# Splitting the AV product of two head pairs around the scores, and one burst's delay for batch 0's stores

## The chip, the cores and the metric

The kernel runs on one core of one Trainium2 chip. The metric is the device time of one execution in microseconds (us), and the figure quoted for a kernel is the median of its runs.

## The reference

For 8 batches, 12 heads, 448 positions and a head size of 64, attention without softmax is followed by a layer norm without bias, a feed-forward block and a residual. Cut to what matters:

```
scores = q @ k.T / sqrt(64)
attn   = maximum(scores, 0)**2 / 448
x      = attn @ v                      # heads side by side: [8, 448, 768]
xn     = (x - mean) / sqrt(var + 1e-6) * g_ln
out    = x + maximum(xn @ w_ch1, 0) @ w_ch2      # 768 -> 3072 -> 768
```

## The kernel before, in words

Heads are worked on in pairs, six pairs to a batch. The 48 pairs are numbered through, so that batch 2 holds pairs 12 to 17. The scores of one pair are made transposed, with keys on the partitions: three full tiles of 128 keys (t = 0, 1, 2) and a rest of 64 keys, the quarter (t = NF = 3). The quarters of two neighbouring pairs share one tile. `att_QK` makes one tile of scores on TensorE and takes it through the relu into SBUF; `att_square` squares it on VectorE; AV then multiplies the squares by v.

The attention of batch b+1 is computed while the feed-forward of batch b runs. `ffn_1_all(b)` makes the 24 hidden tiles (index `ni`) of the first layer, each 12 matmuls into one PSUM bank, taken out by a relu on ScalarE (L424). After chosen tiles, named in `bursts` (for b of 2 and more at ni = 1, 4, 7, 10, 13, 16, 19; for b = 1 two tiles later; for b = 0 `IN_FIRST`), an `excursion(3)` is put in: it makes the scores of the next three tiles of the list `slots`. When both pairs of a neighbouring couple are complete, that excursion begins with their AV: `att_AV2`. This happens twice for each of the seven batches whose attention lies in a feed-forward, so 14 times in a run. The third couple of a batch is finished by single `att_AV` calls.

The order on every engine is the order in which the Python code emits instructions (`tc.manual_schedule`); nothing reorders them. So what is emitted earlier stands earlier in the queue of its engine, and in SyncE's queue of DMA issues too.

[...] Two score tiles `sc0`, `sc1` of two banks each take turns; `f0` and `f1` (`next_f`) take turns for the feed-forward's tiles and for the AV; `f2` and `f3` are `spare`. The profile writes `f` for all four of f0 to f3. The feed-forward tile just ahead of an `att_AV2` goes to `spare[1]` (f3), so that f0 and f1 are both free for the AV sums of the two pairs. The feed-forward tile after the burst goes to the bank of the first pair, the one after that to the bank of the second. The third tile of scores of a burst (m = 2) is put into f2 and f3, half by half, and its relu is done in two instructions (L295): both on VectorE, or for b = 1 the first on ScalarE (L293) and the second on VectorE.

TensorE is used in tiled shapes, which the profile gives behind the operation: 128\*64 for AV full tiles (L317), the feed-forward (L422) and the Strassen-like second layer (L490); 64\*64 for AV quarters (L341) and score quarters (L284); 64\*128 for full score tiles (L289).

Before the change `att_AV2` does the 6 full-tile matmuls of the first pair, the 6 of the second, then 2 quarter matmuls for each; then `av_out` takes the first pair's sum out on VectorE (L351) and the second's on ScalarE (L349). `av_out` also emits an addition into `xs` on VectorE (L358, L360), and for odd pairs the load of v for the next batch.

q and k of batches 2 and up are loaded by GpSimd DMAs into a ring of three (`load_qk`) and turned by a DMA transpose that SyncE issues (`att_T`, L256) into one of three `qkT` buffers. When the last score tile of pair i has been made, `queued(i)` issues the transpose for pair i + 3 and notes the load for pair i + 6; the loads are issued at the start of the next excursion (`flush_loads`). SyncE also issues all the stores of the output (L450). The output of batch 0 is made by plain products, `plain_part`, whose stores are kept in `held_stores`: 4 tiles, each two DMAs, are let out in `ffn_1_all(1)` behind an excursion.

Of the kernel before, what the change touches and what calls it, by code (L numbers as in the profile page):

```python
# [11 lines left out]
def kernel(  # L12
# [10 lines left out]
    nc = tc.nc  # L23
# [14 lines left out]
    NF = S // P  # L38
    SF = NF * P
    SS = S - SF  # L40
# [93 lines left out]
    def v_parts(b):  # L134
        v_sb = v1_sb if b == 1 else v_ring
        return (v_sb[:, :H * NF * D].rearrange("p (h e) -> p h e", h=H),
                v_sb[:, H * NF * D:].rearrange("p (a e) -> p a e", a=NPAIR))
# [21 lines left out]
    def row0(i, hh):  # L159

        return D * ((i + hh) % 2)
# [11 lines left out]
    def load_v(i):  # L173

        b, a = divmod(i, NPAIR)
        v_heads, v_rest = v_parts(b)
        nc.gpsimd.dma_start(v_heads[:, 2 * a:2 * a + 4],
                            v[b, 2 * a:2 * a + 4, :SF].rearrange("h (p t) d -> p h (t d)", t=NF))
        for r0, h0, step in ((0, 0, 3), (D, 1, 1)):
            heads = slice(h0, h0 + step + 1, step)  # L180
            nc.gpsimd.dma_start(v_rest[r0:r0 + SS, a:a + 2, r0:r0 + D],  # L181
                                v[b, 2 * a:2 * a + 4][heads, SF:].rearrange("h s d -> s h d"))
# [33 lines left out]
    attn = {}  # L216
# [4 lines left out]
    def by_j(x):  # L221
        return x.rearrange("p (j s) -> p j s", j=NJ)
# [21 lines left out]
    def q_of(i, r):  # L244
        if i < PE_T * NPAIR:
            return by_j(flat(i)[r, :S])
        return qkT[i][r, :NJ, :SP]

    def k_of(i, r, t, keys):
        c0 = (S if i < PE_T * NPAIR else NJ * P) + t * P  # L250
        return flat(i)[r, c0:c0 + keys]
# [18 lines left out]
            pe_T(i, t, ps)  # L270
        (copy or nc.vector.tensor_copy)(flat(i)[:, :2 * S], ps)

    def att_QK(i, t, relu_by=nc.scalar):

        at = attn_pool.tile([P, 2, S], bf16, tag="attn")
        attn[i, t] = at
        ps = next_sc() if relu_by is nc.scalar else None
        half = [bank[:, :S] for bank in (spare if ps is None else (ps[:, 0], ps[:, 1]))]
        if t == NF:
            for x in range(2):  # L280
                for hh in range(2):
                    r = slice(hh * D, (hh + 1) * D)
                    r0 = row0(i + x, hh)
                    nc.tensor.matmul(by_j(half[x][r0:r0 + SS]), k_of(i + x, r, t, SS), q_of(i + x, r),  # L284
                                     start=True, stop=True)
        else:
            for hh in range(2):
                r = slice(hh * D, (hh + 1) * D)
                nc.tensor.matmul(by_j(half[hh]), k_of(i, r, t, P), q_of(i, r), start=True, stop=True)  # L289
        if ps is None:  # L290
            for x in range(2):
                if relu_by[x] is nc.scalar:
                    nc.scalar.activation(at[:, x], half[x], Act.Relu)  # L293
                else:
                    nc.vector.tensor_scalar(at[:, x], half[x], 0.0, None, op0=Alu.max)  # L295
        else:
            nc.scalar.activation(at, ps[:, :, :S], Act.Relu)  # L297

    def att_square(i, t):
        nc.vector.tensor_mul(attn[i, t], attn[i, t], attn[i, t])  # L300
# [5 lines left out]
    def xT_of(b, ki):  # L306
        return xT[:, ki, (b % 2) * S:(b % 2 + 1) * S]

    def av_part(ps, i, t, start, stop):
        b, pr = divmod(i, NPAIR)  # L310
        v_heads, v_rest = v_parts(b)
        for hh in range(2):
            if t < NF:
                weights, values = v_heads[:, 2 * pr + hh, t * D:(t + 1) * D], attn[i, t][:, hh, :]
            else:
                weights, values = v_rest[:, pr, row0(i, hh):row0(i, hh) + D], attn[i - i % 2, NF][:, i % 2, :]
            nc.tensor.matmul(ps[hh * D:(hh + 1) * D, :], weights, values, start=start, stop=stop)  # L317
# [12 lines left out]
    def att_AV2(i):  # L330

        ps = [next_f()[:, :S] for _ in range(2)]
        for x in range(2):
            for t in range(NF):
                av_part(ps[x], i + x, t, t == 0, False)
        b, pr = divmod(i, NPAIR)
        v_rest = v_parts(b)[1]
        for x in range(2):
            for hh in range(2):
                r0 = row0(i + x, hh)  # L340
                nc.tensor.matmul(ps[x][hh * D:(hh + 1) * D, :], v_rest[r0:r0 + SS, pr + x, r0:r0 + D],  # L341
                                 attn[i, NF][r0:r0 + SS, x, :], start=False, stop=True)
        for x in range(2):
            av_out(i + x, ps[x], (nc.vector, nc.scalar)[x])

    def av_out(i, ps, evac_by):
        b, pr = divmod(i, NPAIR)
        if evac_by is nc.scalar:
            nc.scalar.mul(xT_of(b, pr), ps, c2)  # L349
        else:  # L350
            nc.vector.tensor_scalar(xT_of(b, pr), ps, c2, None, op0=Alu.mult)  # L351
        if i >= PE_T * NPAIR and i % 2 and i + NPAIR < NP_ALL:
            load_v(i - 1 + NPAIR)
        if b == 0:
            if pr < GAIN_FIRST:
                nc.vector.tensor_scalar(xc[:, pr, :], xT_of(b, pr), g_sb[:, pr:pr + 1], None, op0=Alu.mult)
        elif pr == 1:
            nc.vector.tensor_add(xs, xT_of(b, 0), xT_of(b, 1))  # L358
        elif 1 < pr < NPAIR - 1:
            nc.vector.tensor_add(xs, xs, xT_of(b, pr))  # L360
# [101 lines left out]
    held_stores = []  # L462
# [134 lines left out]
    def flush_loads():  # L597
        while loads:
            load_qk(loads.pop(0))

    def queued(i):
        if PE_T * NPAIR <= i + 3 < NP_ALL:
            att_T(i + 3)
            if i + 6 < NP_ALL:
                loads.append(i + 6)
# [12 lines left out]
    ready = []  # L618

    def ends(i, t):  # L620

        if i % 2 == 0:
            return [i] if t == (NF - 1 if i % NPAIR else NF) else []
        return [i] if t == NF - 1 else []

    def next_AV(**how):
        if ready:
            att_AV(ready.pop(0), **how)

    def excursion(n, third=(nc.vector, nc.vector), **how):  # L630
        flush_loads()
        if len(ready) > 1:
            assert ready[0] % 2 == 0 and ready[1] == ready[0] + 1
            att_AV2(ready.pop(0))
            ready.pop(0)
        elif ready and ready[0] % NPAIR == NPAIR - 2:
            next_AV(**how)
        took = [slots.pop(0) for _ in range(n)]
        for m, (i, t) in enumerate(took):
            att_QK(i, t, relu_by=third if m == 2 else nc.scalar)  # L640
        for i, t in took:
            att_square(i, t)
        for i, t in took:
            for e in ends(i, t):
                ready.append(e)
                queued(e)
# [78 lines left out]
    def ffn_1_all(b):  # L725
        ms = tiles_of(b)
        for ni in range(NI0 if b == 0 else 0, K2):
            if b == 0 and ni == NI0:
                ffn_1_first()
            if b == 0 and ni == X_AT[0]:  # L730

                nc.sync.dma_start(held, h[:1, ni - 1, CARRY:CARRY + 16])
            if b == 0 and ni in X_AT:
                ffn_x(b, X_AT.index(ni))
            if b == 0 and ni in V_AT:
                load_v(V_AT[ni])
            bursts = IN_FIRST if b == 0 else [n + (2 if b == 1 else 0) for n in IN_REST]
            ffn_1(ni, spare[1] if b < B - 1 and ni in bursts and len(ready) > 1 else None)
            flush()
            at = STATS_AT[min(b, 2)][:len(ms)]  # L740
            if ni in at:
                ffn_stats(ms[at.index(ni)])
            if b == 1 and ni in SUMS_AT:
                w2_sums(*LATE_SUMS[SUMS_AT.index(ni)])
            if b == 0:
                if ni in IN_FIRST:
                    excursion(3)
                if ni == IN_FIRST[-1] + 3:
                    next_AV(bank=spare[1])
                if ni in T_IN_FIRST:  # L750
                    att_T(NPAIR + T_IN_FIRST[ni])
            elif b < B - 1:
                if ni in bursts:
                    excursion(3, **(dict(third=(nc.scalar, nc.vector), evac_by=nc.scalar) if b == 1 else {}))
                    while ni > bursts[0] and held_stores:
                        held_stores.pop(0)()
                if ni == min(bursts[-1] + 3, K2 - 1):
                    flush_loads()
                    next_AV(bank=spare[1])
# [69 lines left out]
    with tc.manual_schedule(engines=set(ENGINES)):  # L829
# [22 lines left out]
        i = PE_T * NPAIR  # L852
# [41 lines left out]
```

## Time and profile before

| what | value |
|---|---|
| median of 12 runs | 524.38 us (lowest 523.77) |
| profiled execution, its own time | 525.16 us |
| its span in the profile | 523.4 us |
| TensorE matmul busy | 514.5 us (98%) |
| VectorE, ScalarE, GpSimd busy | 368.2, 276.1, 222.6 us |
| granted TensorE clock | 1.0 throughout |

The span runs from the first to the last instruction that the profile shows; 1.8 us of the profiled execution lie outside it. A matmul's end in the profile is modelled, so that "busy" hides small stalls of TensorE: the starts of successive matmuls are the sharper reading. A pair of matmuls in the two halves of a 128\*64 array starts every 0.19 us, although each is shown to take about 0.35 us.

### The profile page before, as it was taken

How to read it: one execution, taken by the hardware profiler on the slowest of the kernel's cores; microseconds unless marked ns; L12 is line 12 of the kernel's file. 1: busy time of each engine (PE TensorE's matmuls, PEld its weight loads, DVE VectorE, ACT ScalarE, POOL GpSimd, SP SyncE). 2: the span in 40 equal slices, each digit the busy share in tenths (PEclk: the TensorE clock that was granted, in tenths of full speed). 3: DMA queues.
4: the chain of work that ended last, by engine and by line, in shares of the span. 5: the costliest groups of instructions: out<-in, count | busy, mean ns of one | idle time of the engine just before them, and what ended most of it. 6: DMA issues, size and time to landing. Idle time of an engine off the chain costs nothing.

```text
span 523.4 us, 13642 instructions
## 1 busy us (share of the span) xinstructions
PE 514.5 (98%) x5705; PEld 318.8 (61%) x5705; DVE 368.2 (70%) x650; ACT 276.1 (53%) x456; POOL 222.6 (43%) x255
## 2 busy tenths in 40 slices
PE   8999999999999999999999999999999999999996
PEld 4445566556765566655787556655666556665665
DVE  5966779778958669587685867787695866951255
ACT  6985643776247652476624766476524765234320
POOL 8727116667523853238532386237532000320031
PEclk9999999999999999999999999999999999999999
DMA  9999999999645992659924599369924300250022
GB/s 141 189 196 203 184 202 164 179 135 107 88 103 73 130 91 63 121 63 130 92 62 105 64 126 137 77 73 119 93 68 100 59 4 3 62 116 7 1 54 69
DMA packets 175261, 53.03 MB, mean 101 GB/s; under 512 B 154208, under 2 KB 175200, under 8 KB 175200
## 3 DMA queue, kind: packets, MB, share of 16 engines
q0 software_dynamic: 103552, 25.74, 53.0%
q1 hardware_dynamic: 71120, 26.06, 27.2%
q8 instruction: 44, 0.72, 0.6%
q10 hardware_dynamic: 528, 0.37, 0.2%
q14 instruction: 17, 0.14, 0.1%
HBM read 51.91 MB, written 11.01 MB: 120 GB/s over the span
## 4 chain that ended last, share of the span: by engine, by line
PE 90%; DVE 5%; DMA 2%; ACT 1%; POOL 1%; issue 0%; POOLq 0%; DVEq 0%
PE f L422 41%; PE f L490 34%; PE f L317 5%; PE f L473 3%; PE sc L289 3%; DVE xT L351 2%; DVE at L300 2%; PE f L289 1%; DMA qkT_t<-qk_ring 1%; DMA w<-in_k_dram 1%; PE f L341 1%; PE f L708 1%; PE f L232 1%; PE f L381 1%; ACT at L297 0%; PE sc L284 0%
## 5 line engine op out<-in xcount | busy, mean ns | idle before, releaser
L422 PE MATMUL f<-xc,w 128*64 128x448 bf16 x2256 | 225.9, 353 | 1.6
L422 PEld LDWEIGHTS <-w 128*64 128x64 bf16 x2256 | 131.5, 110 | 90.3 <-issue 18.7
L424 ACT ACTIVATE h<-f 128x448 bf16<-128x448 f32 x188 | 102.8, 547 | 98.3 <-PE f L422 97.4
L490 PE MATMUL f<-w,s_sb 128*64 128x384 bf16 (+2 forms) x1584 | 130.0, 324 | 0.0
L490 PEld LDWEIGHTS <-s_sb 128*64 128x64 bf16 x1584 | 92.9, 110 | 34.4
L297 ACT ACTIVATE at<-sc 128x896 bf16<-128x896 f32 x120 | 103.3, 918 | 5.0 <-PE sc L289 4.8
L300 DVE TENSOR_TENSOR at<-at 128x896 bf16<-128x896 bf16 x168 | 95.5, 618 | 4.3 <-ACT at L297 4.1
L523 POOL TENSOR_TENSOR o_t<-o_t,x_tok 128x384 f32<-128x384 f32 x26 | 24.4, 938 | 151.6 <-ACT o_t L522 151.6
L169 POOL DMA_DIRECT2D qk_ring<-in_q_dram x36 | 44.5, 1236 | 89.2 <-DMA qkT_t<-qk_ring 63.5
L295 DVE TENSOR_SCALAR at<-f 128x448 bf16<-128x448 f32 x89 | 51.6, 618 | 26.9 <-PE f L289 26.9
L522 ACT ACTIVATE o_t<-f,rstd 128x384 f32<-128x384 f32 x26 | 15.1, 582 | 94.6 <-DVE acc_t L527 35.8
L484 DVE TENSOR_TENSOR s_sb<-h 128x1536 bf16<-128x1536 bf16 x65 | 64.1, 1002 | 0.0
L170 POOL DMA_DIRECT2D qk_ring<-in_k_dram x36 | 53.5, 1487 | 11.0 <-DMA w<-in_moe_w_ch_dram 11.0
L490 PE MATMUL f<-w,h 128*64 128x384 bf16 x624 | 52.9, 326 | 0.0
L171 POOL DMA_DIRECT2D qk_ring<-in_k_dram x36 | 43.9, 1220 | 5.7 <-DMA w<-in_moe_w_ch_dram 4.7
L490 PEld LDWEIGHTS <-h 128*64 128x64 bf16 x624 | 36.9, 110 | 14.1
L351 DVE TENSOR_SCALAR xT<-f 128x448 bf16<-128x448 f32 x33 | 20.4, 619 | 32.3 <-PE f L341 21.8
L523 POOL TENSOR_TENSOR acc_t<-acc_t,x_tok 128x384 f32<-128x384 f32 x24 | 28.9, 1211 | 22.3 <-ACT acc_t L522 21.2
L181 POOL DMA_DIRECT2D v_ring<-in_v_dram x36 | 34.7, 1331 | 0.0
L317 PE MATMUL f<-at,v_ring 128*64 128x448 bf16 x288 | 33.8, 354 | 0.5 <-DVE xT L351 0.3
L388 DVE SCALAR_TENSOR_TENSOR xc<-f,g_sb,xc 128x448 bf16<-128x448 f32 x45 | 28.5, 678 | 6.7 <-PE f L381 6.0
L289 PE MATMUL sc<-qkT_t 64*128 64x448 bf16 x192 | 30.0, 356 | 0.0
(87 smaller groups left out, 394.9 us busy)
## 6 DMA issues: line engine op xcount, KB each, us to landing
w<-in_moe_w_ch_dram POOLq DMA_DIRECT2D x6, 768.0 KB, 12.8
w<-in_moe_w_ch_dram POOLq DMA_DIRECT2D x4, 1152.0 KB, 29.3
v_ring<-in_v_dram POOLq DMA_DIRECT2D x21, 192.0 KB, 5.3
qk_ring<-in_q_dram POOLq DMA_DIRECT2D x36, 112.0 KB, 4.9
qk_ring<-in_k_dram POOLq DMA_DIRECT2D x36, 96.0 KB, 5.0
out_dram<-o_t SPq DMA_DIRECT2D x8, 168.0 KB, 2.2
out_dram<-acc_t SPq DMA_DIRECT2D x7, 168.0 KB, 2.2
out_dram<-o_t SPq DMA_DIRECT2D x8, 144.0 KB, 2.1
```

Of the source, the lines that this page charges most:

```text
L169: nc.gpsimd.dma_start(q_to, q[b, heads].rearrange("x (p j) d -> p j x d", j=NJ))
L170: nc.gpsimd.dma_start(k_to[:, :NF], k[b, heads, :SF].rearrange("x (p t) d -> p t x d", t=NF))
L289: nc.tensor.matmul(by_j(half[hh]), k_of(i, r, t, P), q_of(i, r), start=True, stop=True)
L295: nc.vector.tensor_scalar(at[:, x], half[x], 0.0, None, op0=Alu.max)
L297: nc.scalar.activation(at, ps[:, :, :S], Act.Relu)
L300: nc.vector.tensor_mul(attn[i, t], attn[i, t], attn[i, t])
L317: nc.tensor.matmul(ps[hh * D:(hh + 1) * D, :], weights, values, start=start, stop=stop)
L422: nc.tensor.matmul(ps[c * D:(c + 1) * D, :], w1[:, ki, n0:n0 + D], xc[:, ki, :], start=(ki == 0), stop=(ki == K1 - 1))
L424: nc.scalar.activation(h[:, ni, CARRY:], ps, Act.Relu)
L484: nc.vector.tensor_tensor(s_sb[:, n], x, y, op=op)
L490: nc.tensor.matmul(ps[c * D:(c + 1) * D, :d1 - d0], stat[:, ki, c * D:(c + 1) * D], w2[:, slot, ki, d0:d1], start=(start and ki == 0), sto ...
L523: nc.gpsimd.tensor_tensor(o_t, o_t, x_half(m, dh), op=Alu.add)
```

## The change

Of the two pairs in `att_AV2`, only the first gets its full tiles ahead of the quarters. The quarters of both pairs follow; for the second pair they now begin the sum (`start` is set for x = 1) where they ended it. The first pair's sum is taken out by ScalarE. The rest, the second pair's 6 full-tile matmuls and its `av_out` on VectorE, is returned as a function. The excursion hands it to the `att_QK` of its third tile, which calls it between the two relu instructions. So TensorE does the second pair's full tiles behind all three score tiles, and VectorE takes the sum out between the two halves of the relu.

Apart from that, in `ffn_1_all(1)` the held stores of batch 0 come behind the third burst (ni = 9), where they came behind the second (ni = 6).

```diff
-    def att_QK(i, t, relu_by=nc.scalar):
+    def att_QK(i, t, relu_by=nc.scalar, between=None):
...
                     nc.vector.tensor_scalar(at[:, x], half[x], 0.0, None, op0=Alu.max)
+                if x == 0 and between:
+                    between()
...
     def att_AV2(i):

         ps = [next_f()[:, :S] for _ in range(2)]
-        for x in range(2):
-            for t in range(NF):
-                av_part(ps[x], i + x, t, t == 0, False)
+        for t in range(NF):
+            av_part(ps[0], i, t, t == 0, False)
...
                 nc.tensor.matmul(ps[x][hh * D:(hh + 1) * D, :], v_rest[r0:r0 + SS, pr + x, r0:r0 + D],
-                                 attn[i, NF][r0:r0 + SS, x, :], start=False, stop=True)
-        for x in range(2):
-            av_out(i + x, ps[x], (nc.vector, nc.scalar)[x])
+                                 attn[i, NF][r0:r0 + SS, x, :], start=x == 1, stop=x == 0)
+        av_out(i, ps[0], nc.scalar)
+
+        def rest():
+            for t in range(NF):
+                av_part(ps[1], i + 1, t, False, t == NF - 1)
+            av_out(i + 1, ps[1], nc.vector)
+
+        return rest
...
     def excursion(n, third=(nc.vector, nc.vector), **how):
         flush_loads()
+        rest = None
         if len(ready) > 1:
             assert ready[0] % 2 == 0 and ready[1] == ready[0] + 1
-            att_AV2(ready.pop(0))
+            rest = att_AV2(ready.pop(0))
...
         for m, (i, t) in enumerate(took):
-            att_QK(i, t, relu_by=third if m == 2 else nc.scalar)
+            att_QK(i, t, relu_by=third if m == 2 else nc.scalar, between=rest if m == 2 else None)
...
-                    while ni > bursts[0] and held_stores:
+                    while ni > bursts[1] and held_stores:
                         held_stores.pop(0)()
```

## The prediction

> **What bounds the kernel now.** I read the page first (who is busy, what the chain that ended last consists of), then the chain in order of time, then the timeline of single bursts, and last SyncE's timeline, because the change also moves stores.
>
> ```profile
> span 523.4 us, 13642 instructions
> ...
> PE 514.5 (98%) x5705; PEld 318.8 (61%) x5705; DVE 368.2 (70%) x650; ACT 276.1 (53%) x456; POOL 222.6 (43%) x255
> ...
> PEclk9999999999999999999999999999999999999999
> ...
> PE 90%; DVE 5%; DMA 2%; ACT 1%; POOL 1%; issue 0%; POOLq 0%; DVEq 0%
> ...
> L422 PE MATMUL f<-xc,w 128*64 128x448 bf16 x2256 | 225.9, 353 | 1.6
> ```
>
> TensorE is the bound, at full clock. Yet 5% of the chain is VectorE. About half of that lies in the first 27 us, where batch 0's attention has no feed-forward beside it; the rest has one recurring form:
>
> ```profile
> 166.55 1.14 PE f L317 x12
> 168.10 0.64 DVE xT L351
> 168.78 3.60 PE f L422 x36
> ```
>
> AV, then the first pair's sum taken out by VectorE, then the feed-forward. The chain passes over the scores, which TensorE does meanwhile. The timeline of that burst shows why:
>
> ```profile
> 166.38 1.30 PE L317 MATMUL f<-at,v_ring 128*64 128x448 bf16 x12
> ...
> 167.61 0.38 PE L341 MATMUL f<-at,v_ring 64*64 64x448 bf16 x4
> ...
> 168.07 0.54 ACT L349 ACTIVATE xT<-f 128x448 bf16<-128x448 f32 x1 [0.94 <-PE f L341]
> 168.10 0.62 DVE L351 TENSOR_SCALAR xT<-f 128x448 bf16<-128x448 f32 x1 [1.12 <-PE f L341]
> ...
> 168.31 0.35 PE L289 MATMUL f<-qkT_t 64*128 64x448 bf16 x2
> ...
> 168.60 3.35 PEld L422 LDWEIGHTS <-w 128*64 128x64 bf16 x36 [0.37 <-issue]
> 168.78 3.60 PE L422 MATMUL f<-xc,w 128*64 128x448 bf16 x36
> ```
>
> The weights of the first feed-forward matmul are in at 168.60, but it starts at 168.78, 0.06 us after VectorE is done with its bank (168.72). From the last score matmul to it are 0.47 us. In the next burst, without two pairs' AV, they are 0.29 us:
>
> ```profile
> 172.69 0.35 PE L289 MATMUL f<-qkT_t 64*128 64x448 bf16 x2
> ...
> 172.98 0.57 PE L422 MATMUL f<-xc,w 128*64 128x448 bf16 x4
> ```
>
> Through the whole trace this step from L289 to L422 takes 0.279 to 0.29 us 35 times and 0.459 to 0.462 us exactly 14 times: the 14 calls of `att_AV2`. The list of waits misses it, because the modelled end of the score matmul covers most of it; the 1.6 us of idle time in the L422 row is the remainder, 14 × 0.12.
>
> One more stall of TensorE after the start is a single one, in the feed-forward of batch 1, where a score tile waits for the transpose of pair 16:
>
> ```profile
> 94.73 1.24 SPq L256 DMA_TRANSPOSE qkT_t<-qk_ring  x1
> 96.06 3.25 SPq L450 DMA_DIRECT2D out_dram<-o_t  x4
> 99.40 3.35 SPq L450 DMA_DIRECT2D out_dram<-acc_t  x4
> 103.32 1.23 SPq L256 DMA_TRANSPOSE qkT_t<-qk_ring  x1
> ```
>
> ```profile
> 109.47 0.36 PE L289 MATMUL f<-qkT_t 64*128 64x448 bf16 x2 [0.69 <-DMA qkT_t<-qk_ring]
> ```
>
> That transpose was due when pair 13's last scores were made, at about 99. It stood behind batch 0's eight stores on SyncE, went out at 103.32 and landed at 109.42; TensorE's start-to-start gap there is 1.04 us where 0.19 is usual.
>
> **The change part by part.** *The split.* All instructions stay, 16 AV matmuls and two evacuations. In the burst above the first pair's AV starts at 166.38, 166.57 and 166.75, the quarters at 167.04, the scores in f2 and f3 at 167.74 (all 0.57 earlier than now, three steps of 0.19), the second pair's full tiles at 168.03, 168.22 and 168.40, and the feed-forward at 168.59, if its bank is free. ScalarE can begin to take out the first pair 0.46 us behind the quarters' start (as 167.61 to 168.07 now), at 167.50, and is done at 168.05: 0.5 us early. So the wait goes: 14 × (0.461 − 0.280) = 2.5 us.
>
> Whether the split costs drains is where I weigh a rule. In the trace a change of the array's shape takes 0.28 us start to start (L317 to L341, L289 to L422) against 0.19 inside one shape. The Trainium skill, page "TensorEngine Tiling (Array Packing)", Key Properties, says that switching the tiling mode drains TensorE; read against this change, two groups of AV in place of one are two more drains of 0.1 us, 14 times, 2.8 us, and the gain would be eaten. But the second group stands directly ahead of the feed-forward, which has its shape: 128\*64, 64\*64, 64\*128, 128\*64 before and after, three switches each. I take nothing.
>
> *What is late next.* The second pair's bank is wanted by the second feed-forward tile, six steps on, at 169.71. VectorE can begin on it about 0.43 us behind the last AV start (in the burst at 119.10 the last AV start is 119.66, the evacuation at 120.09), so at 168.83; with 0.62 and 0.06 the bank is free at 169.51, 0.2 us early. Ahead of it on VectorE's queue stands the first half of the relu, from 168.13 (0.39 behind its matmul); the next instruction follows 0.53 later, in time. For pairs 2 and 3 of a batch there is also an `xs` addition, released by ScalarE's evacuation at about 168.09; a following instruction starts 0.31 later, so the relu starts at 168.40, the evacuation at 168.93, and the bank is free 0.1 us early. Behind the waiting evacuation stand the `xs` addition, the second half of the relu and three squares. They end about 0.2 us later than now, near 172.1, and their first reader is the AV at 176.41. If VectorE were later, every 0.1 us past this slack costs 14 × 0.1. Bounds: nothing to 0.1 us each, 1.4 us; I take nothing, since the rows leave the slack.
>
> ScalarE gets the first evacuation 0.57 earlier, and its two relus of scores, waiting behind the evacuation now too, earlier as well. In the feed-forward of batch 1, where it also does half of the third relu, its hidden relu is late now: two feed-forward steps two tiles behind an AV burst take 0.27 instead of 0.19. Those 2 × 0.08 = 0.2 us should go. GpSimd's load of v, released by the second pair's last matmul, becomes possible at 168.8 in place of 168.1; GpSimd gets to it at 170.74 because of the loads of q and k ahead of it, so it costs nothing.
>
> *The stores.* Behind the third burst, the transpose of pair 16 stands ahead of them. It needs the scores of pair 13 (99) and its loads (landed by 96.5), so it can go at about 99; with the 6.1 us of today or even the 7.7 of the one before it, it lands by 105 to 107, ahead of 108.6, where it is wanted. Gain 1.04 − 0.19 = 0.85 us; bounds 0 and 0.85, and I take the upper one. The eight stores then fill SyncE from 100 to about 106, the transpose of pair 17 behind them (105.15 now) goes about then, lands near 111 and is wanted at 120. The stores' tiles are wanted again only by the second layer at 123.7. One thing comes nearer: the transpose of pair 15 landed at 102.41, its reader at 103.63 will come 0.57 + 2 × 0.18 earlier, at 102.7. At most a few tenths could come back here.
>
> Sum: 2.5 + 0.2 + 0.85 = 3.5 us. The profiled execution's 525.16 becomes 521.7; it lies 0.8 above the median, so the median goes from 524.38 to 520.9.
>
> **The rivals.** *The transpose or the stores fail me* (wait not gone, or one elsewhere): against it speak the 1.7 us and more of margin above, for it a crowded DMA (173 GB/s in 94 to 104). Gain 2.7 at most, 521.7.
>
> *VectorE's evacuation becomes the wait, a little.* For it: 0.1 us of slack in seven of the bursts. At 0.1 us past the slack in all 14, gain 2.1, 522.3; at 0.2, 523.6.
>
> *It becomes the wait by much, and the kernel is slower.* One queue: VectorE, the evacuation between two relu halves. It decides at 0.1 to 0.2 us of lateness; past 0.4 us (3.5 / 14 = 0.25 beyond the slack) all is lost. One more instruction ahead of it, statistics or a sum of w2 of 1.35 us still running, would do: 1.0 us late is 14 × 0.85 − 3.5 = 8.4 us, 532.8. Against it: VectorE sat idle for 1.12 us ahead of that evacuation, and statistics are placed at other tiles.
>
> *Additional drains,* so that the change does not bring what it removes: 2.5 − 2.8 for the split, 523.6 in all. The order of shapes speaks against it.
>
> **How the numbers follow.** All as worked out 0.68 (520.9, by itself 520.3 to 521.5); the transfers fail 0.12 (521.7); a small wait on VectorE 0.12 (522.3 to 523.6); drains 0.03 (523.6); slower 0.05 (532.8). 0.5%, 2.6 us, is about what a measurement of this kernel can tell from no change. Faster by more: nearly all of the first, half of the second, a little of the third, 0.75. Within it: 0.19. Slower by more: 0.06, with something for what I have not seen. The range of 520.1 to 523.0 takes in the first two and the better half of the third.
>
> **What would show it.** Right: the step from the AV's 128\*64 matmuls to L422's first is 0.19 behind each split AV, no step of 0.46 is left, the chain has no evacuation between AV and feed-forward, the gap at 109 is gone, the transpose of pair 16 goes at about 99. Wrong: a gap at the second feed-forward tile behind such a burst, ended by VectorE's evacuation; a new wait on `qkT_t` in 100 to 125; more than three steps of 0.28 in a burst.

## The result and the profile after

The changed kernel takes 522.26 us (median of 12 runs, 521.44 to 524.06); the kernel before took 525.01 us (median of 48 runs, the 12 runs of its own table among them; 523.77 to 529.48, and one of 1272.68 that nothing here explains) in the same comparison. The ratio of after to before is 0.9941, 95% interval [0.9921, 0.996]. By the medians 2.75 us are saved, where 3.5 were forecast (520.9 us, from a median of 524.38). The ratio says a little more than the medians, whose quotient is 0.9948: a quarter of the executions before lie more than 1 us above their median, and the means (522.43 and 525.56, without the one execution) are 3.1 us apart. The gain is clear of the noise and a little smaller than worked out.

The profiled execution took 523.95 us, 1.7 above the median, and it shows what was gained and what was lost. First the page and the list of TensorE's waits, of the changed kernel (L317, L341 and L351 of before are now L319, L342 and L358; ScalarE's evacuation is L356, the first layer L429):

```profile
span 522.2 us, 13617 instructions
...
PE 94%; DVE 3%; DMA 1%; ACT 1%; issue 0%
...
L429 PE MATMUL f<-xc,w 128*64 128x448 bf16 x2256 | 225.4, 353 | 0.1
...
PE sc L284 <- DMA qkT_t<-qk_ring: 1.5, 1, 1.5
```

VectorE's share of the chain has gone from 5% to 3%, with no evacuation between AV and feed-forward left in it, and the feed-forward's idle time (L422 before, L429 now) from 1.6 to 0.1 us. A wait of 1.5 us for a transpose is new. The burst that the prediction followed looks like this now (timeline; start, duration, engine, line):

```profile
166.92 0.73 PE L319 MATMUL f<-at,v_ring 128*64 128x448 bf16 x6
...
167.59 0.38 PE L342 MATMUL f<-at,v_ring 64*64 64x448 bf16 x4
...
168.00 0.54 ACT L356 ACTIVATE xT<-f 128x448 bf16<-128x448 f32 x1 [0.33 <-PE f L342]
...
168.29 0.35 PE L289 MATMUL f<-qkT_t 64*128 64x448 bf16 x2
...
168.57 0.76 PE L319 MATMUL f<-at,v_ring 128*64 128x448 bf16 x6
168.68 0.62 DVE L295 TENSOR_SCALAR at<-f 128x448 bf16<-128x448 f32 x1 [1.15 <-PE f L289]
...
169.16 3.57 PE L429 MATMUL f<-xc,w 128*64 128x448 bf16 x36
169.44 0.62 DVE L358 TENSOR_SCALAR xT<-f 128x448 bf16<-128x448 f32 x1
```

From the first AV matmul to the feed-forward are 2.24 us (166.92 to 169.16); before they were 2.40 (166.38 to 168.78). ScalarE has emptied the first pair's bank by 168.54, 0.6 us ahead of need. No step of 0.46 us is left in the whole trace. VectorE empties the second bank by 170.06. TensorE followed an evacuation by 0.06 us in the trace before (168.72 to 168.78), which leaves 0.17 us to the second feed-forward tile at 169.16 + 6 × 0.188 = 170.29.

And this is where 1.8 us went in this execution, in the feed-forward of batch 1 (TensorE, then SyncE's issues):

```profile
103.00 0.35 PE L284 MATMUL sc<-qkT_t 64*64 64x448 bf16 x2
104.83 0.38 PE L284 MATMUL sc<-qkT_t 64*64 64x448 bf16 x2 [1.48 <-DMA qkT_t<-qk_ring]
```

```profile
95.00 2.08 SPq L409 DMA_TRANSPOSE x_tok<-xT  x1
98.49 4.57 SPq L256 DMA_TRANSPOSE qkT_t<-qk_ring  x2
103.16 2.01 SPq L457 DMA_DIRECT2D out_dram<-o_t  x4
```

The two transposes at 98.49 are those of pairs 15 and 16. Pair 16's goes out at 100.89, ahead of the stores, and its wait is gone. Pair 15's went out 3.8 us later than in the trace before (94.73) and landed at 104.79, with its reader waiting since 103.0. The stores stand behind it and cannot have held it up.

### The profile page after: what moved, and what is told of

Its sections match the earlier page's. It is cut to its first block, busy times and chain, and to the rows that moved or that the text cites. A ratio compares the mean times of both kernels' runs of the same rounds, so it can differ in the third digit from the quotient of the medians.

```text
span 522.2 us, 13617 instructions
## 1 busy us (share of the span) xinstructions
PE 514.5 (99%) x5705; PEld 312.4 (60%) x5705; DVE 368.2 (71%) x650; ACT 277.1 (53%) x456; POOL 222.6 (43%) x255
## 4 chain that ended last, share of the span: by engine, by line
PE 94%; DVE 3%; DMA 1%; ACT 1%; issue 0%
PE f L429 41%; PE f L497 34%; PE f L319 5%; PE sc L289 4%; PE f L480 3%; PE f L289 2%; DVE at L302 2%; DMA qkT_t<-qk_ring 1%; PE f L598 1%; PE sc L284 1%; PE f L232 1%; PE f L342 1%; PE f L716 1%; DVE xT L358 1%; PE f L388 1%; DVE qkT_t L271 0%
## 5 line engine op out<-in xcount | busy, mean ns | idle before, releaser
L429 PE MATMUL f<-xc,w 128*64 128x448 bf16 x2256 | 225.4, 353 | 0.1
L429 PEld LDWEIGHTS <-w 128*64 128x64 bf16 x2256 | 125.6, 110 | 91.8 <-issue 13.3
L299 ACT ACTIVATE at<-sc 128x896 bf16<-128x896 f32 x120 | 103.0, 919 | 6.6 <-PE sc L289 5.0
L169 POOL DMA_DIRECT2D qk_ring<-in_q_dram x36 | 47.4, 1316 | 92.5 <-DMA qkT_t<-qk_ring 68.1
L295 DVE TENSOR_SCALAR at<-f 128x448 bf16<-128x448 f32 x89 | 52.7, 619 | 30.7 <-PE f L289 30.7
L170 POOL DMA_DIRECT2D qk_ring<-in_k_dram x36 | 56.1, 1559 | 12.5 <-DMA w<-in_moe_w_ch_dram 12.5
L171 POOL DMA_DIRECT2D qk_ring<-in_k_dram x36 | 47.6, 1322 | 4.8 <-DMA w<-in_moe_w_ch_dram 4.6
L319 PE MATMUL f<-at,v_ring 128*64 128x448 bf16 x288 | 36.1, 357 | 0.4 <-DVE xT L358 0.3
L181 POOL DMA_DIRECT2D v_ring<-in_v_dram x36 | 32.3, 1201 | 0.0
L358 DVE TENSOR_SCALAR xT<-f 128x448 bf16<-128x448 f32 x33 | 20.3, 617 | 15.9 <-PE f L319 15.0
```

Source lines behind the costliest of these rows:

```text
L170: nc.gpsimd.dma_start(k_to[:, :NF], k[b, heads, :SF].rearrange("x (p t) d -> p t x d", t=NF))
L171: nc.gpsimd.dma_start(k_to[:SS, NF], k[b, 2 * a:2 * a + 2, SF:].rearrange("x s d -> s x d"))
L429: nc.tensor.matmul(ps[c * D:(c + 1) * D, :], w1[:, ki, n0:n0 + D], xc[:, ki, :], start=(ki == 0), stop=(ki == K1 - 1))
```

## Which part brings what

**The split alone.**

```diff
-                    while ni > bursts[1] and held_stores:
+                    while ni > bursts[0] and held_stores:
```

> The split alone; batch 0's stores stay behind the second burst. If the split removes the wait for the first pair's bank and costs no drains (my theory): no step of 0.46 us from L289 to the feed-forward is left, 14 x 0.181 + 0.2 = 2.7 us less than before, ratio about 0.9948; the single gap at the transpose of pair 16, 0.7 to 0.9 us, is still there or has moved to pair 15. If the split is paid for in drains: no gain, ratio about 1.000. If the stores were what mattered: ratio above 0.998.

Measured: 522.37 us against 525.18, ratio 0.9951 [0.9931, 0.997]. No step of 0.46 us is left, so the theory of the bank holds and that of the drains does not. The split also exchanges the two engines that empty the banks, and no run tests that exchange by itself. In the burst of the trace before, ScalarE was done at 168.61 and VectorE at 168.72; an estimate from these two is that ScalarE on the first pair's bank would by itself have taken 0.11 of the 0.18 us off the step. The wait for pair 16 was there, and larger than I had expected:

```profile
PE f L289 <- DMA qkT_t<-qk_ring: 2.5, 1, 2.5
```

In this profiled execution (524.78 us, 2.4 above the kernel's median) the stores ran from 97.56 to 103.47 on SyncE, the transpose of pair 16 went at 103.84 and landed at 111.07.

**The stores alone.**

```diff
-                    while ni > bursts[0] and held_stores:
+                    while ni > bursts[1] and held_stores:
```

> The stores alone, one burst later; AV of both pairs ahead of the scores as before. As predicted: the 14 steps of 0.46 us stay, the gap at the transpose of pair 16 goes, ratio 0.9984 (0.85 us). Rival, from the trace of the changed kernel: moving the stores makes the transpose of pair 15 late (TensorE waited 1.5 us for it there), then the ratio is 1.000 to 1.002 and the trace shows a wait on qkT_t near 103. If the late transpose of pair 15 is a matter of the moment and not of the stores, it may be absent here.

Measured: 524.68 us against 525.18, ratio 0.9977 [0.9961, 0.9993]. The 14 steps of 0.459 to 0.462 us stayed. SyncE's timeline shows the new order:

```profile
95.16 5.32 SPq L256 DMA_TRANSPOSE qkT_t<-qk_ring  x2
100.58 2.22 SPq L450 DMA_DIRECT2D out_dram<-o_t  x4
102.90 2.89 SPq L450 DMA_DIRECT2D out_dram<-acc_t  x4
```

Pair 16's transpose went at 99.22 and landed at 105.46; TensorE waited for no transpose. Pair 15's landed at 103.12, its reader came at 103.44: 0.3 us of margin, and moving the stores did not make it late.

What the later stores do shows best in the spread, all in one session: 16 of the 57 runs of the kernel before lie more than 1 us above their median, and 5 of 16 with the split alone, but none of these 22 and none of 10 of the changed kernel. By the means the stores alone save 0.9 us (525.61 to 524.67), by the medians 0.5. That the long runs are runs with a long wait for pair 16 is likely (the profiled one of the split alone was 2.4 us above its median with 2.65 us of such waiting) but not shown for the others.

**The kernel before, a second trace.**

> The kernel before once more, for a second trace. The 14 steps of 0.46 us are fixed by the order and must be there again; the gap at the transpose of pair 16 depends on the DMA's timing and may be 0 to 2.6 us (0.85 in the first trace, 2.65 with the split alone).

The 14 steps were there again, 0.459 to 0.462 us. The gap at pair 16 was not: its transpose went out at 103.53, much as before, and landed at 108.72, ahead of its reader at 109.09; in the first trace it landed at 109.42, 0.8 behind the 108.62 at which its reader was due. So what I had read off one trace as a fixed 0.85 us is there in some executions only.

**The changed kernel again, three times.**

> The changed kernel once more, unaltered. If the wait of 1.5 us for the transpose of pair 15 belongs to the change, it is in this trace too, within 0.3 us. If it comes and goes with the DMA's timing, it is absent or of another size here, and the spread of the runs (521.4 to 524.1) is explained by it. Ratio again 0.992 to 0.996.

> The changed kernel a third time, on the same chip as the kernel with the other order of transposes. Wait for the transpose of pair 15: present in one of two traces so far. If it is an edge (landing 103.0 against a reader at 103.0 to 103.2), here it is between 0 and 2 us. Ratio 0.992 to 0.996.

> The changed kernel a fourth time, on the same chip as its two variants, to compare them with. Ratio 0.993 to 0.996; wait for the transpose of pair 15 0 to 2 us.

Ratios 0.9935 [0.991, 0.996], 0.9957 [0.994, 0.9974] and 0.9946 [0.9928, 0.9964]. Laid beside each other, the traces separate what the order decides from what the DMA decides. The stages are cut at the first matmul of each (us):

| trace | feed-forward of batch 0 | of batch 1 | everything from batch 1's second layer on | pair 15's transpose landed | gap at its reader |
|---|---|---|---|---|---|
| before | 34.30 | 39.16 | 399.69 | 102.41 | none (0.85 at pair 16) |
| before, again | 34.30 | 38.29 | 399.75 | 103.03 | none |
| stores alone | 34.30 | 38.30 | 399.70 | 103.12 | none |
| split alone | 33.94 | 40.83 | 397.94 | 103.14 | 0.43 (2.84 at pair 16) |
| changed | 33.93 | 39.76 | 397.94 | 104.79 | 1.82 |
| changed, again | 33.93 | 37.71 | 397.90 | 102.97 | none |
| changed, third | 33.93 | 38.97 | 397.94 | 104.16 | 0.96 |
| changed, fourth | 33.93 | 38.19 | 397.89 | 103.34 | 0.46 |

(The last column is start to start on TensorE, in a group of four quarter matmuls that else start together; the 0.85 and the 2.84 are between score tiles, the 0.85 without the 0.19 that is usual there.) The first and third stages repeat to 0.1 us: the split is worth 0.37 us in batch 0 (two bursts) and 1.8 us in the last stage (ten bursts), 0.18 us a burst in every trace. Only batch 1's feed-forward scatters, over 2 us for the same program. Without a late transpose it takes 37.71 us with the split, and 38.29 without. What the gap in the last column leaves unexplained of the changed kernel's traces, 0.2 us in the first and 0.3 in the third, stands two bursts on, at the quarter of pairs 16 and 17: pair 17's transpose landed at 114.83 and 114.28 there, at 111.59 in the trace without a wait.

It is the split that brings pair 15's reader nearer, not the stores. The quarter that reads it starts 19.09 us behind the first matmul of batch 1's feed-forward in the three traces without the split and 18.52 in the five with it, the 0.57 us of the forecast. The transpose landed at 103.12 with the stores alone, without a wait, and at 103.14 with the split alone, with one of 0.43 us.

## Is VectorE's evacuation close behind

```diff
-                if x == 0 and between:
+                if x == 1 and between:
                     between()
```

> As the changed kernel, but VectorE takes the second pair's sum out behind both halves of the relu, one instruction of 0.53 us later in its queue; TensorE's order is unchanged. In the trace of the changed kernel the bank is free about 0.17 us before the second feed-forward tile wants it. If that slack is all there is: TensorE waits there 0.1 to 0.4 us in 12 of the 14 bursts (in batch 1's feed-forward ScalarE does the first half), 2 to 4 us in all, ratio 0.998 to 1.002. If there is more slack than I read, it stays at 0.993 to 0.995.

Measured: 525.3 us against 524.99, ratio 0.9988 [0.9967, 1.0009]; the changed kernel in the same session had 523.01. One instruction more ahead of the evacuation, and the split's gain is eaten. Timeline of TensorE and of VectorE in the second couple's burst of one batch:

```profile
178.58 1.30 PE L429 MATMUL f<-xc,w 128*64 128x448 bf16 x12
180.04 2.46 PE L429 MATMUL f<-xc,w 128*64 128x448 bf16 x24 [0.16 <-DVE xT L358]
```

```profile
178.31 1.15 DVE L295 TENSOR_SCALAR at<-f 128x448 bf16<-128x448 f32 x2
179.37 0.61 DVE L358 TENSOR_SCALAR xT<-f 128x448 bf16<-128x448 f32 x1
```

The evacuation now begins behind two relus and ends at 179.98; the second feed-forward tile starts 0.06 later. Its step is 0.51 us in six bursts (pairs 2 and 3 of a batch, where an `xs` addition stands ahead as well) and 0.30 in six, where 0.19 is usual: 6 × 0.32 + 6 × 0.115 = 2.6 us. The two bursts in batch 1's feed-forward, where ScalarE does the first half, show nothing. That is the range that was expected from a slack of 0.17 us. The place between the two halves is therefore part of what makes the split pay.

## What a change of the array's shape costs

```diff
             rest = att_AV2(ready.pop(0))
             ready.pop(0)
+            rest = rest()
```

> The second pair's full tiles directly behind the quarters, ahead of the scores; all else as in the changed kernel. TensorE then goes through the shapes 128*64, 64*64, 128*64, 64*64, 64*128, 128*64 in each of the 14 bursts: five switches in place of three. If a switch costs what the step of 0.28 against 0.19 shows, this is 14 x 2 x 0.095 = 2.7 us slower than the changed kernel, about as fast as before (ratio 0.999). If switches cost nothing by themselves: as fast as the changed kernel (0.994). If a switch costs a full drain of 0.28: 1.004.

Measured: 525.19 us against 525.18, ratio 0.9985 [0.9971, 0.9999]; the changed kernel in the same session had 522.42. Here the second pair's full tiles stand between two groups of 64\*64:

```profile
165.80 0.38 PE L342 MATMUL f<-at,v_ring 64*64 64x448 bf16 x4
166.11 0.76 PE L319 MATMUL f<-at,v_ring 128*64 128x448 bf16 x6
166.80 0.38 PE L284 MATMUL sc<-qkT_t 64*64 64x448 bf16 x4
167.12 0.36 PE L289 MATMUL sc<-qkT_t 64*128 64x448 bf16 x2
167.31 0.35 PE L289 MATMUL f<-qkT_t 64*128 64x448 bf16 x2
167.60 3.60 PE L429 MATMUL f<-xc,w 128*64 128x448 bf16 x36
```

The banks are free in time here too (no step of 0.46 us), and yet nothing is left of the gain by the medians: two more switches of shape, 14 times, cost 2.8 us, 0.1 each. The stages, where no transpose was waited for, say a little more: 34.42 us in batch 0 and 400.41 in the last stage, 0.25 us a burst above the changed kernel, 0.12 a switch. The steps had said about that, 0.28 to 0.31 us where the shape changes against 0.19 to 0.21. The Trainium skill ("TensorEngine Tiling (Array Packing)", Key Properties) says that switching the mode drains TensorE; the traces agree that a switch costs, and show its price, not what happens in it. The change escapes it because its second group stands at the feed-forward, which has its shape.

## The late transpose of pair 15

Pair 15's transpose needs the load of pair 15, whose place in the ring comes free when pair 12's transpose has landed. In the trace before that was at 85.82, in the changed kernel's first trace at 88.86, in its second at 86.35, and the load went out 0.57 to 0.58 us behind it each time. SyncE issues the six transposes of batch 1's tokens in between, while the loads are under way. In the changed kernel's first trace the load landed at 98.34 and the transpose went out at 98.49: there this chain held it up. In the other traces of the table it went out at 94.73 to 95.93 and took 7.2 to 8.5 us to land, so that the chain does not settle the landing: with pair 12's at 88.03 (before, again) pair 15's came at 103.03, with 88.26 (changed, third) at 104.16. Three trials to get it out of the way:

**Transposes of pairs 12 to 14 behind the tokens'** (`queued` keeps the calls for i = 9, 10, 11 back until batch 1's `ffn_x` calls are emitted).

```diff
         if PE_T * NPAIR <= i + 3 < NP_ALL:
+            if i < PE_T * NPAIR and not late.get("done"):
+                late.setdefault("i", []).append(i)
+                return
             att_T(i + 3)
...
                     for ki in range(K1):
                         ffn_x(1, ki)
+                    late["done"] = True
+                    for i in late["i"]:
+                        queued(i)
```

> The changed kernel, with SyncE's transposes of pairs 12 to 14, and the loads that follow them, emitted behind the six transposes of batch 1's tokens instead of ahead of them. If the wait for the transpose of pair 15 comes from the row of transposes and loads that pile up behind 81 us, pair 15's transpose goes out at its scores' end (94) and lands before 100, no trace and no run has the wait, the runs spread by under 1 us, ratio 0.990 to 0.994. If the pile-up only moves (tokens late for the statistics, weights of the second layer late), the trace shows a new wait in 68 to 110 and the ratio is 0.994 or above.

Measured: 527.54 us against 524.99, ratio 1.0045 [1.0031, 1.0058], slower than before. The rival was right, the pile-up only moved:

```profile
PE f L480 <- DMA w<-in_moe_w_ch_dram: 3.2, 3, 2.5
...
PE sc L289 <- DMA qkT_t<-qk_ring: 1.1, 1, 1.1
```

The tokens' transposes now ran while the second layer's weights came in, TensorE waited 3.2 us for those, and pair 12's transpose landed at 95.66. Batch 0's second layer took 21.19 us where 15.98 are usual.

**Two bursts of batch 1's feed-forward one tile later.**

```diff
-            bursts = IN_FIRST if b == 0 else [n + (2 if b == 1 else 0) for n in IN_REST]
+            bursts = IN_FIRST if b == 0 else [3, 6, 9, 13, 16, 18, 21] if b == 1 else IN_REST
```

> The changed kernel, with the fourth and fifth bursts of batch 1's feed-forward one tile (1.13 us) later, at ni = 13 and 16. The reader of pair 15's transpose then comes at about 104.2 in place of 103.1, against landings of 102.4 to 104.8 so far. If that transpose is what the changed kernel still loses (0, 0.77 and 1.64 us in its three traces), the wait is 0 to 0.6 us, and the kernel is 0.3 to 0.9 us faster than the changed one on this chip. If the shorter distance of the fifth and sixth bursts costs as much on ScalarE, it is equal or slower.

Measured: 522.39 us against 524.85, ratio 0.9945 [0.9929, 0.9961]; the changed kernel in the same session 522.29 us. The wait for pair 15 is gone from the trace, its reader coming at about 104.3 against a landing at 103.18. But batch 1's feed-forward took 38.13 us, as in the changed kernel's fourth trace. A new step of 0.41 us stands at 101.16, between two feed-forward tiles: ScalarE, behind three relus of scores, had finished the hidden relu of the tile before last only at 101.11. Another 0.15 us was lost at the quarter of pairs 16 and 17, pair 17's transpose landing at 113.15. What was taken away at one place came back at others.

**The shared quarter one score tile later, in batch 2 alone.**

```diff
-        if i % NPAIR == 2:
+        if i % NPAIR == 2 and i != 2 * NPAIR + 2:
```

> The changed kernel, with pair 14's third full score tile ahead of the shared quarter, in batch 2 alone, so that the reader of pair 15's transpose comes one score tile later (0.3 us). One burst has another switch's worth of shapes (0.1 us). If the transposes decide: 0.2 us faster on average than the changed kernel, hardly to be told; wait for pair 15 0.3 us smaller in the trace. If not: equal.

Measured: 522.83 us against 524.85, ratio 0.9953 [0.9935, 0.9971], not to be told from the changed kernel's 522.29. The transpose landed at 103.77 in this trace, and the step at its reader, 0.39 us later in the stage than in the changed kernel, was still 0.34 us.

None of the three beats the changed kernel, and nor does the split alone (522.37 us against 522.42 in one session): by the medians these two are equal.

## Why the prediction was right, and where it was off

The measured time lies in the range, and the split's mechanism is as described. But the main account, 3.5 us, was not met in full: the 2.75 us by the medians are what the first rival named (the transfers fail, 2.7 us at most, given 0.12), and one of the signs of being wrong, a new wait on `qkT_t` in 100 to 125, was there in three of four traces. That the range held although the stores brought less than forecast is due to the rival having been counted into it.

- *The wait for the first pair's bank, 2.5 us:* right. 0.18 us a burst in every trace with the split; the 14 steps of 0.46 us stand in every trace without it. The split alone gives 0.9951. The burst shown was worked out at 2.21 us from its first AV matmul to the feed-forward, and took 2.24.
- *Drains, nothing:* right, and shown by the kernel that does have two more switches a burst (2.8 us by the medians).
- *VectorE's evacuation keeps a slack of 0.1 to 0.2 us:* right in size. 0.17 was measured in the burst shown, where 0.2 was worked out. In the bursts with an `xs` addition ahead, where 0.1 was worked out, it was 0.20 (evacuated by 179.89 in the burst after, the tile at 180.15), because the addition began 0.05 us earlier in the burst than worked out and the tile came 0.05 later. One more instruction ahead of it costs 2.6 us.
- *ScalarE's late relu, 0.2 us:* right. The two steps of 0.27 us behind batch 1's bursts are not in the changed kernel's traces.
- *The stores, 0.85 us at the upper bound, "a few tenths" given back by pair 15:* this is the term that was mis-sized. The wait for pair 16 goes, in every trace with the later stores; but it was 0.85 in one trace of the kernel before and absent in the other, so that the upper bound was not there in every execution. And pair 15's wait, which I had seen coming from a margin of 0.3 us, was 0.46, 0.96 and 1.82 us in three of four traces of the changed kernel. With 2.7 us for the split and ScalarE, 0.4 for pair 16 (the mean of two traces) and 0.9 lost at pairs 15 and 17 (the mean of four), the sum is 2.2 us; the medians of the four comparisons say 2.0 to 2.8. Between the two kernels with the split, stores and transposes come out even by the medians (522.37 us without the later stores, 522.42 with them) and 0.5 us apart by the means (522.83 and 522.33). Moving the stores alone gave 0.9977 [0.9961, 0.9993]. So what the later stores bring shows most clearly as fewer long executions.
- *"One more stall of TensorE after the start is a single one":* not quite. A step of 0.42 us between two feed-forward tiles stands at 92.38 in the trace before, where a hidden relu of ScalarE ended at 92.33, behind three relus of scores. It is in every trace but that of the transposes behind the tokens', with 0.41 or 0.42 us, and the change does not touch it.

Only inferred is the chain behind pair 15: one trace shows its load holding it up, in the others most of the delay lies between its issue and its landing, and the trial to break the chain broke other things. Why pair 12's transpose takes 4.6 us in one execution and 7.4 in another, and pair 15's 6.3 to 8.5, stays open.

## What to carry to other kernels

Read the steps between the starts of successive matmuls, by pair of lines: a stall that the modelled ends hide shows there as a second value that occurs a fixed number of times. When work is moved to hide a wait, put it next to work of its own array shape, and work out whose bank it now holds and how long that engine's queue can be late. A wait for a DMA seen in one trace may differ in the next: take a second trace before it goes into a sum, and compare the spread of the runs and not their medians alone.

## What I had not expected

The same program differed from trace to trace by up to 2.1 us within 40 us of one stage, at full clock, and by under 0.1 us in the 398 us behind it. The landing of one transpose moved from 102.97 to 104.79 among four traces of the same kernel; the scatter of that stage stood at its reader and, for 0.2 to 0.3 us, at the reader of the next but one.
